# W_in in two parts behind the taps' maximum, block 1's x behind block 0's casts, block 2's first taps on GpSimd

## The chip, the cores and the metric

One core of one Trainium2 chip runs the whole kernel. The metric is the device time in microseconds (us) of one execution.

## The reference, cut to what matters

A causal convolution with seven softmaxed taps per head along the sequence, then a feed-forward layer with exact GELU:

```python
w = softmax(weight)                       # 8 heads x 7 taps
out[b, s, h, :] = sum_k w[h, k] * x_pad[b, s + k, h, :]     # x: 8 x 4096 x 192, 24 columns a head
h = out.reshape(32768, 192) @ w_in        # 192 x 2048
return gelu(h) @ w_out                    # 2048 x 192
```

## The kernel before

Tokens are cut into blocks: six of 256 per half of the sequence, then 512. For each block x is loaded (four DMAs of 96 KB), VectorE transposes it in three parts and applies seven taps (the first a `tensor_scalar`, the other six `scalar_tensor_tensor` with two SBUF inputs), TensorE multiplies by W_in in eight chunks (12 matmuls and one GELU each), ScalarE does the GELU, TensorE multiplies by W_out. Blocks 0 and 1 get their taps on TensorE instead, as matmuls with diagonal matrices that VectorE builds first ("the diagonals"). GpSimd casts, and copies the halo: the few columns that a block needs of the one before. The prologue loads everything through the same 16 DMA engines (from 4 to 5 us of the profile before, W_in's queue took 64.6% of their time and x's 34.3%): block 0's x, W_in (cast to bf16 by GpSimd's DMA queue), block 1's x, W_out, block 2's x.

```python
FP = [0, FQ, 2 * FQ, FH]                  # W_in in three parts: 256, 256, 512 columns of each half
...
# GpSimd
for i in range(3):
    win_in(FP[i], FP[i + 1], S_WIN[i])    # two DMAs each, at once
...
# TensorE, chunk i of block n
if u >= 2: t.wait_ge(S_GELU, u - 1)
...
if n == 0 and i < 3:
    t.wait_ge(S_WIN[i], 32)
...
# the DMA-issuing engine
load(sp, 0, (0, 1))
sp.wait_ge(S_WIN[0], 32)
load(sp, 1)
for i in range(4): ...                    # W_out
load(sp, 2)
load(sp, 3)
```

## Time and profile before

| | value |
|---|---|
| time, median of 3 runs | 683.07 us (682.57 to 683.39) |
| span of the profiled run | 681.6 us |
| TensorE busy | 674.2 us, 99% |
| first matmul of block 2 | 29.91 us |

The lines that bear the argument stand in the prediction. Two more are from the timeline of the kernel before: start, length, engine, line, operation, and in brackets the idle time before it and what ended it.

```profile
9.85 1.27 PE L756 MATMUL hp<-xc,win 64*128 64x256 bf16 x20 [0.17 <-ACT xc L191]
...
21.76 0.88 DVE L548 TENSOR_SCALAR acc<-xT,wcol 128x256 f32<-128x256 f32 x3
22.55 6.02 DVE L555 SCALAR_TENSOR_TENSOR acc<-xT,wcol,acc 128x256 f32<-128x256 f32 x15
```

TensorE runs from its first chunk into its second without waiting for W_in. The fifteen later taps begin at 22.55 us and end at the start of the last three, 28.49, so one comes every 0.396 us, and the third of them starts at 22.55 + 2 x 0.396 = 23.34 us.

### The profile page before, as it was taken

The numbers are of one execution on the slowest core, as the hardware profiler recorded it, in microseconds if no ns is written. First come the engines' busy times: TensorE is split into PE (matmuls) and PEld (weight loads), VectorE is DVE, ScalarE is ACT, GpSimd is POOL, SyncE is SP. The second block draws the span as 40 slices with busy tenths as digits, with TensorE's granted clock in tenths as the row PEclk, the third lists the DMA queues.
The fourth block names the chain that finished last, engine by engine and source line by source line (L and its number), as shares of the span: only waits on it lengthen the run. The fifth ranks groups of instructions, "written<-read, shape, count | busy, mean of one in ns | idle before, by whom it ended". The sixth has DMA issues, their size and how long they took to land.

```text
span 681.6 us, 27311 instructions
## 1 busy us (share of the span) xinstructions
PE 674.2 (99%) x12572; PEld 410.2 (60%) x12572; DVE 560.9 (82%) x908; ACT 536.5 (79%) x548; POOL 38.6 (6%) x57
## 2 busy tenths in 40 slices
PE   7999999999999999999999999999999999999998
PEld 4899755555555555555555555555555555555557
DVE  6899989888889888898888898888898888988611
ACT  6799988877787877777877778777778777778772
POOL 5025100000000000000000000000000000000000
PEclk9999999999999999999999999999999999999999
DMA  9436332234432143432234322334322334221123
GB/s 196 92 101 130 72 71 72 42 78 95 96 93 52 47 95 94 95 73 52 68 94 95 94 64 46 83 94 96 93 48 51 95 94 96 72 46 27 48 50 94
DMA packets 133890, 54.45 MB, mean 80 GB/s; under 512 B 127504, under 2 KB 133776, under 8 KB 133776
## 3 DMA queue, kind: packets, MB, share of 16 engines
q1 hardware_dynamic: 131408, 51.33, 32.0%
q8 instruction: 98, 1.61, 1.0%
q0 software_dynamic: 1248, 0.79, 0.9%
q10 hardware_dynamic: 1120, 0.59, 0.3%
q14 instruction: 16, 0.13, 0.1%
HBM read 28.31 MB, written 25.17 MB: 78 GB/s over the span
## 4 chain that ended last, share of the span: by engine, by line
PE 95%; DMA 2%; DVE 1%; SPq 1%; issue 0%; POOL 0%
PE hp L756 47%; PE ob L818 43%; PE ob L786 5%; DMA xin<-in_x_dram 1%; DVE acc L555 1%; PE hp L786 1%; SPq L330 1%; DMA win<-in_moe_w_in_dram 1%; SPq L882 0%; DVE xT L522 0%; DVE acc L548 0%; DVE xc L555 0%; POOL win L385 0%; POOL idb L393 0%; DVE osb L283 0%
## 5 line engine op out<-in xcount | busy, mean ns | idle before, releaser
L677 ACT ACTIVATE gT<-hp 128x1024 bf16<-128x1024 f32 x512 | 523.1, 1024 | 129.7 <-PE hp L756 126.4
L756 PE MATMUL hp<-xc,win 64*64 64x512 bf16 (+2 forms) x6048 | 419.5, 366 | 2.2 <-DVE xc L555 1.1
L818 PE MATMUL ob<-gT,wout 64*64 64x512 bf16 x5376 | 366.3, 376 | 0.0
L555 DVE SCALAR_TENSOR_TENSOR acc<-xT,wcol,acc 128x512 f32<-128x512 f32 (+1 forms) x495 | 315.3, 708 | 0.0
L756 PEld LDWEIGHTS hp<-xc,win 64*64 64x64 bf16 (+1 forms) x6048 | 189.9, 106 | 135.2 <-ACT gT L677 3.1
L818 PEld LDWEIGHTS ob<-gT,wout 64*64 64x64 bf16 x5376 | 172.0, 118 | 123.0
L314 DVE STREAM_TRANSPOSE osb<-ob 128x512 f32<-128x512 f32 x84 | 74.2, 886 | 100.3 <-PE ob L818 100.3
L522 DVE STREAM_TRANSPOSE xT<-xin 128x512 f32<-128x512 f32 (+1 forms) x105 | 78.4, 807 | 4.5 <-DMA xin<-in_x_dram 4.5
L555 DVE SCALAR_TENSOR_TENSOR xc<-xT,wcol,acc 128x512 bf16<-128x512 f32 (+1 forms) x99 | 65.4, 720 | 0.0
L447 POOL COPY xT<-xT 128x18 f32<-128x18 f32 x30 | 27.9, 930 | 505.0 <-DVE xT L522 482.7
L786 PE MATMUL ob<-wout,gT 64*128 64x192 bf16 x896 | 47.8, 243 | 0.0
L786 PEld LDWEIGHTS ob<-wout,gT 64*128 64x128 bf16 x896 | 40.0, 94 | 3.9 <-issue 0.4
L548 DVE TENSOR_SCALAR acc<-xT,wcol 128x512 f32<-128x512 f32 (+1 forms) x90 | 37.6, 474 | 1.1
L691 PE MATMUL hp<-warm 128*128 128x512 bf16 x12 | 5.1, 616 | 1.3 <-DVE warm L463 1.3
L285 ACT ACTIVATE osb<-ob 128x192 f32<-128x192 f32 x2 | 0.7, 331 | 7.1 <-PE ob L786 7.1
L786 PE MATMUL hp<-wout,gT 64*128 64x192 bf16 x128 | 5.9, 243 | 0.0
L283 DVE COPY osb<-ob 128x192 f32<-128x192 f32 x2 | 0.7, 358 | 6.1 <-PE ob L786 6.1
L786 PEld LDWEIGHTS hp<-wout,gT 64*128 64x128 bf16 x128 | 5.3, 94 | 0.0
L650 ACT ACTIVATE acc<-xT,wcol 128x256 f32<-128x256 f32 (+1 forms) x9 | 5.2, 575 | 0.0
L270 ACT ACTIVATE osb<-ob 128x384 f32<-128x384 f32 x10 | 4.9, 490 | 0.0
L707 PE MATMUL ob<-xTb,dg 64*64 64x256 bf16 (+1 forms) x112 | 3.2, 245 | 1.1 <-ACT xTb L626 1.1
L193 DVE CAST xc<-ob 64x256 bf16<-64x256 f32 (+3 forms) x8 | 2.8, 357 | 1.5 <-PE ob L707 1.4
(36 smaller groups left out, 29.9 us busy)
## 6 DMA issues: line engine op xcount, KB each, us to landing
out_dram<-osb SPq DMA_DIRECT2D x122, 192.0 KB, 3.1
xin<-in_x_dram SPq DMA_DIRECT2D x116, 192.0 KB, 4.1
xin<-in_x_dram SPq DMA_DIRECT2D x22, 96.0 KB, 4.3
woutf<-in_moe_w_out_dram SPq DMA_DIRECT2D x4, 384.0 KB, 6.2
win<-in_moe_w_in_dram POOLq DMA_DIRECT2D x4, 96.0 KB, 3.8
win<-in_moe_w_in_dram POOLq DMA_DIRECT2D x2, 192.0 KB, 5.5
out_dram<-osb SPq DMA_DIRECT2D x8, 48.0 KB, 1.7
out_dram<-osb ACTq DMA_DIRECT2D x4, 96.0 KB, 1.9
```

Source lines behind the costliest of these rows:

```text
L314: v.transpose(ap(osb[m % 2], j, [[8 * C, 128], [C // 2, TB // 32], [NP, 32]]), bank(ring(m, j)),).then_inc(S_EV)
L330: e.dma_start(ap(xin[n % NX], 32 * q * (TB // 32 * DQ), dst), ap(xt, off, src)).then_inc(sm or S_XIN[n % NX], 16)
L447: g.tensor_copy(dst, src).then_inc(S_HALO)
L522: v.transpose(ap(xT[n % 2], p * XW + HX, [[NP * XW, 128], [1, w]]), ap(xin[n % NX], p, [[TB // 32 * DQ, 128], [DQ, w // 32], [NP, 32]],),) ...
L548: ins = v.tensor_scalar(a, src, wk, None, ALU.mult)
L555: ins = v.scalar_tensor_tensor(dst, src, wk, a, op0=ALU.mult, op1=ALU.add)
L650: a.activation(out=acc[n % 2][:, p * TB : p * TB + w], in_=ap(xT[n % 2], p * XW + HX, [[NP * XW, 128], [1, w]]), func=AF.Copy, scale=wcol[ ...
L677: a.activation(out=ap(gT[n % 2], i * c * 2 * w, dst), in_=ap(hp[u % 2], 0, src), func=AF.Gelu,).then_inc(S_GELU)
L691: t.matmul(hp[1][:, 0:512], warm[:, 0:128], warm[:, :])
L756: ins = t.matmul(hp[u % 2][fo : fo + fw, o : o + w], ap(win, f1, [[NP * F, 64], [2, fw]]), xc[n % 2][r, p * TB : p * TB + w], start=(p == ...
L786: ins = t.matmul(bb[sub], gT[m % 2][r, c0 : c0 + 128], wout[r, CH[sub][i] * C : (CH[sub][i] + 1) * C], start=(ph == 0 and i == 0), stop=(p ...
L818: ins = t.matmul(bank(ring(m, j), slice(64 * h, 64 * h + 64), w), ap(wout, 64 * hf * NF * C + CH[h][i] * C + j, [[NF * C, 64], [NP, 64]],) ...
```

## The change

Its intent: let block 0's x have the DMA engines to itself at first (W_in's load waits for `S_PRO`, that is, until VectorE has taken the maximum of the taps, its first step of their softmax), keep block 1's x out of W_in's way, and take three instructions off VectorE, which sets block 2's start.

```diff
-        S_WIN = [sem("S_WIN%d" % i) for i in range(3)]
+        S_WIN = [sem("S_WIN%d" % i) for i in range(2)]
-        FP = [0, FQ, 2 * FQ, FH]
+        FP = [0, FQ, FH]
 # GpSimd
-                    for i in range(3):
+                    g.wait_ge(S_PRO, 1)
+                    for i in range(2):
                         win_in(FP[i], FP[i + 1], S_WIN[i])
...
             for n in range(2, NB):
                 halo(n)
+                if n == KG:               # KG = 2
+                    for p in range(NP):
+                        g.wait_ge(S_TR, NP * n + p + 1)
+                        g.tensor_scalar(acc[...], xT[...], wcol[:, KS - 1 : KS], None, ALU.mult).then_inc(S_KG)
 # VectorE: block KG starts at its second tap
-                if k == h and h:
+                if k == h and n == KG:
+                    v.wait_ge(S_KG, p + 1)
+                elif k == h and h:
 # TensorE
-                if n == 0 and i < 3:
+                if n == 0 and i < 2:
                     t.wait_ge(S_WIN[i], 32)
 # the DMA-issuing engine
-            sp.wait_ge(S_WIN[0], 32)
+            sp.wait_ge(S_CAST[0], NP)
             load(sp, 1)
```

(Cut: the counting of semaphores, GpSimd's wait for the column of taps, and VectorE's wait for the part of W_in that it copies. The call of `tensor_scalar` is shortened.)

More of the change, by code (lines that the diff above doesn't have):

```diff
@@ L36, in bass_lightweight_conv__then__act_gelu_exact_kernel @@
     K0 = {4: 0, 5: 1, 6: 2}
+    KG = 2
     NA = 5
@@ L163, in bass_lightweight_conv__then__act_gelu_exact_kernel @@
         S_K0 = sem("S_K0")
+        S_KG = sem("S_KG")
         block = es.enter_context(nc.Block())
@@ L218, in cvd @@
         def cvd(n):
-            return sum(NCV - NP * (m in K0) for m in range(n + 1) if m not in PC)
+            return sum(NCV - NP * (m in K0 or m == KG) for m in range(n + 1) if m not in PC)
         HC = [0]
@@ L457, in _ @@
                 g.tensor_copy(wout[:, o : o + 4 * C], woutf[:, o : o + 4 * C]).then_inc(S_WOG)
+            g.wait_ge(S_PRO, 9)
             for n in range(2, NB):
                 halo(n)
+                if n == KG:
+                    for p in range(NP):
+                        g.wait_ge(S_TR, NP * n + p + 1)
+                        g.tensor_scalar(
+                            acc[n % 2][:, p * TB : p * TB + WS[n]],
+                            ap(xT[n % 2], p * XW + HX, [[NP * XW, 128], [1, WS[n]]]),
+                            wcol[:, KS - 1 : KS],
+                            None,
+                            ALU.mult,
+                        ).then_inc(S_KG)
         @block.vector
@@ L498, in dup @@
             def dup(s):
-                v.wait_ge(S_WIN[min(s, 2)], 32)
+                v.wait_ge(S_WIN[min(s, 1)], 32)
                 for hf in range(2):
@@ L532, in conv @@
                 w = WS[n]
-                h = int(n in K0)
+                h = int(n in K0 or n == KG)
                 if k == h and p == 0:
@@ L564, in _ @@
                 ops = [] if n in K0 else [("t", n, p) for p in range(NP)]
-                ops += [("c", n, k, p) for k in range(int(n in K0), KS) for p in range(NP)]
+                ops += [("c", n, k, p) for k in range(int(n in K0 or n == KG), KS) for p in range(NP)]
                 if n + 1 in K0:
```

## The prediction

The two terms of its 0.33 us were: about 0.7 us gained if VectorE's later taps run on beside GpSimd's first taps (its "free case", one chance in three), 0.15 if they have to wait for them. Both terms and the chances were estimates, from the times of the taps before (21.76 to 22.55 us) and of GpSimd's taps at 0.45 to 0.5 us each, ending at 22.31 to 22.45. The sum came to 29.91 - 0.33 = 29.58 us for the start of block 2, and so to 682.7 us.

> **What bounds the kernel now.** The page first. It shows an engine that is never free.
>
> ```profile
> PE 674.2 (99%) x12572; PEld 410.2 (60%) x12572; DVE 560.9 (82%) x908; ACT 536.5 (79%) x548; POOL 38.6 (6%) x57
> ...
> PE 95%; DMA 2%; DVE 1%; SPq 1%; issue 0%; POOL 0%
> ```
>
> TensorE is busy for 674.2 of 681.6 us and owns 95% of the chain that ended last. The change touches no matmul, so at most the few us in which TensorE is idle are to be had. Next, who TensorE waited for, over the whole span:
>
> ```profile
> PE hp L691 <- DVE warm L463: 1.3, 1, 1.3
> PE hp L756 <- DVE xc L555: 1.1, 1, 1.1
> PE ob L707 <- ACT xTb L626: 1.1, 1, 1.1
> PE hp L756 <- ACT gT L677: 0.7, 2, 0.5
> PE hp L756 <- ACT xc L191: 0.3, 2, 0.2
> ```
>
> That is the complete list: 4.5 us, all of it in the first 30 us. After 29.91 us TensorE never waits again. So the end moves one for one with the moment at which TensorE starts block 2, and I read only the first 30 us. The chain in order of time, with start, length and what:
>
> ```profile
> 13.02 7.33 DMA xin<-in_x_dram
> 20.37 1.36 DVE xT L522 x3
> ...
> 22.64 4.82 DVE acc L555 x13
> ...
> 29.29 0.49 DVE xc L555
> 29.77 0.14 issue
> 29.91 0.83 PE hp L756 x12
> ```
>
> Block 2's x lands at 20.35 us, VectorE transposes it (1.36 us), does 21 tap instructions, and TensorE starts at 29.91. The timeline of TensorE shows how much this wait is worth:
>
> ```profile
> 28.13 0.66 PE L786 MATMUL ob<-wout,gT 64*128 64x192 bf16 x12
> 29.91 0.29 PE L756 MATMUL hp<-xc,win 64*128 64x256 bf16 x2 [1.12 <-DVE xc L555]
> ```
>
> TensorE is out of work at 28.79 us, 1.12 us earlier. There are thus two paths into 29.91: block 2's (DMA, VectorE), and TensorE's own work on blocks 0 and 1, only 1.12 us shorter. Shortening the first alone gains at most 1.1 us; more needs both shortened.
>
> [...] GpSimd's halo copy of 128x18, 0.31 us when it met first taps or transposes, took 3.56 us at 40.36 us and 11.92 us at 58.14 us, beside runs of later taps. [...] GpSimd's cast takes 0.441 us for 256 columns and 0.826 for 768, a slope of 0.75 ns per column over about 0.25 us. [...] the W_in and x queues share the same engines. The trace agrees: from 4 to 5 us W_in's queue took 64.6% of them and x's 34.3%.
>
> **The change part by part.**
>
> *W_in after the maximum, in two parts.* GpSimd now begins its issues at 2.00 us. The maximum starts at 2.17 and lasts 0.15, so W_in is issued from about 2.35, 0.35 us later. Its packets begin at about 4.0 us now, while block 0's x still has 161 packets to move from 4 to 5 us and 52 from 5 to 6 us. At the 551 packets per us of the slice 3 to 4 us, those 213 take 0.4 us alone. So x of block 0 can land some 0.3 to 0.6 us before its 6.33 us, and no transfer time is lost, as the engines stay full; earlier than 5.25 us helps nothing, as VectorE is busy with the diagonals until then. I take 0.4. Two issues of about 0.65 us go, but the engines, not the issues, are the limit: W_in's 0.79 MB moves at 0.11 to 0.17 MB per us until about 10.5 us either way.
> The price is coarseness. Now piece 1 is there by about 8.4 us (issued from 3.3, 3.7 to 4.3 us to land) and the last piece by 11.2 (5.27 + 5.9). With two parts TensorE's second chunk of block 0 (about 10.2 us now) waits for all of the rest, about 11.0 us. The five gelus from 10.51 us run back to back, each 0.99 us; the second would then start at 11.7 instead of 11.5. Block 0's head start of 0.4 us is spent here, and a further 0.2 may be lost.
>
> *Block 1's x behind the casts.* Its issue waited for W_in's first part (6.64 us); it will wait for ScalarE's third cast, which ends at 8.14 now and at 7.75 if x lands 0.4 earlier: 1.1 us later. But its packets didn't flow from 6.66 on: x's queue moved one packet from 6 to 9 us, W_in all the rest. They moved from 9 to 12 us. Issued 1.1 us later they find W_in nearly done. I expect block 1's x at 13.1 us instead of 12.74. GpSimd's casts of it end 1.5 us after landing for the second third, and TensorE's taps (14.30 us) waited 0.21 us for just that cast, so they follow: TensorE's own path ends at 28.79 + 0.4 = 29.2 us.
> W_out and block 2's x are issued behind it, about 1.1 us later too. Block 2's x was issued 7.3 us before it landed; it stood in a queue that was over 90% full from 3 to 20 us. The same bytes through the same full engines: I leave 20.35 us, plus or minus 0.5.
>
> *First taps on GpSimd.* Three VectorE instructions go. They stood from 21.76 to 22.55 us, so up to 0.79 us, if the later taps may start at once. GpSimd, as with block 1's casts (0.59 us after the first transpose begins, then 0.45 each), would run them at 20.96, 21.41 and 21.86 and end at 22.31; with fp32 output and a scalar per partition perhaps 0.5 each, ending at 22.45. VectorE's first later tap is ready at 21.76, in the middle. [...] I give the free case one chance in three: 0.33 x 0.7 + 0.67 x 0.15 = 0.33 us.
> The later taps cost the same: 18 at 0.40 us.
>
> *Sum.* Block 2's path: 29.91 - 0.33 = 29.58. TensorE's path: 29.2. The later one counts: 29.58, a gain of 0.33 us, so 683.07 - 0.33 = 682.7 us. Block 3 follows on VectorE without a break (its last tap ends at 40.30, TensorE wants it at 40.44), so the same gain is passed on, no more.
>
> **The rivals.** *1: all as intended.* The casts and taps on GpSimd overlap cleanly, block 2's x lands 0.3 us earlier. For it: engines full, bytes the same. Against it: the 11.92 us halo copy. Then 29.91 - 0.79 - 0.3 = 28.82 and TensorE's path at 29.2 becomes the bound: 682.4; with that path also shorter by its 0.4 us head start, 681.9. *2: block 1's x is the new wait.* It lands 1.1 us later, as it is issued; TensorE's path then ends at 29.9, and the time stays at 683.1 whatever GpSimd does. For it: TensorE waited for exactly this cast. Against it: the queue's idle time from 6 to 9 us. *3: GpSimd's taps are slow*, 0.7 us each and shut out by VectorE: the third ends at about 23.8, the third later tap starts 0.4 us later than now: 683.5. *4: W_out slips.* Its last part landed at 18.8 us, and TensorE wants it, cast (0.83 us), at about 20.5: 1 us of slip makes TensorE wait and delays GpSimd's first taps, 683.6.
>
> **Range and chances.** The middle is 682.7. Rival 1 at 681.9 and rivals 3 and 4 at 683.6 bound it, and the runs before spread over 0.8 us by themselves: 681.8 to 683.7 should hold it 8 times in 10. A change of 2% is 13.7 us. All idle time of TensorE together is 4.5 us, so faster by 2% isn't possible, and a loss of that size would need a stall in the steady part, which the change doesn't touch: 0.01 for each.
>
> **What would show it.** In the changed profile: transposes of block 0 start at about 5.95 us rather than 6.35; block 0's second gelu starts near 11.7; block 1's transposes start near 13.1, block 2's near 20.4; the three GpSimd taps take about 0.5 us each, with a wait of VectorE's first or third later tap for them; TensorE's wait before block 2 shrinks from 1.12 us to about 0.4; no new wait of TensorE after 31 us. I am wrong if block 2's x lands over 0.6 us away from 20.35, if the GpSimd taps take over 0.7 us, or if TensorE's wait moves to block 1's taps or to W_out.

## The result, and the profile after

The changed kernel took 684.06 us in the median of 6 runs (682.97 to 685.06), the kernel before 683.34 in 6 runs beside it. The ratio is 1.0012, 95% interval 0.9999 to 1.0025: 2% is far off either way, but 684.06 lies outside the predicted 681.8 to 683.7, and the small change points the other way than predicted. That it is a loss at all is nearly, not quite, clear of noise: the interval just includes no change, and so does that of the same kernel in e9, 1.0007 (0.9994 to 1.0019). (A ratio is the mean time of one kernel's fast runs over that of the other's of the same rounds, so not quite the ratio of the medians quoted.)

The profiled run took 683.77 us, with a span of 682.0. First again who TensorE waited for, in the changed kernel; columns as in the prediction: total, times, longest.

```profile
PE hp L774 <- DMA win<-in_moe_w_in_dram: 1.5, 1, 1.5
PE hp L709 <- DVE warm L479: 1.3, 1, 1.3
PE hp L774 <- DVE xc L573: 0.9, 1, 0.9
PE hp L774 <- ACT xc L194: 0.5, 2, 0.3
PE hp L774 <- ACT gT L695: 0.5, 1, 0.5
```

The wait for ScalarE's cast of block 0 (1.1 us before) is gone, as intended. A wait of 1.5 us for W_in has taken its place, and the wait before block 2 is still 0.9. The chain in order of time shows why that one remains:

```profile
20.32 0.54 DVE xT L538
...
20.95 0.77 POOL acc L469
...
21.87 1.82 POOL acc L469 x2
...
23.72 4.12 DVE acc L573 x11
...
30.29 0.83 PE hp L774 x12
```

Block 2's x is there at 20.30 us, as before, and as predicted. But VectorE now waits for GpSimd: the three taps end at 23.69, and VectorE's third later tap starts at 23.72 instead of 23.34. TensorE starts block 2 at 30.29 instead of 29.91, 0.38 us later. The end follows: span less start of block 2 is 682.0 - 30.29 = 651.71, before 681.6 - 29.91 = 651.69. In this profile the GpSimd taps account for the whole 0.4 us by which its span is longer. The timeline shows the GpSimd taps, and VectorE beside them:

```profile
20.95 2.73 POOL L469 TENSOR_SCALAR acc<-xT,wcol 128x256 f32<-128x256 f32 x3 [1.22 <-DVE xT L538]
...
22.02 0.59 DVE L573 SCALAR_TENSOR_TENSOR acc<-xT,wcol,acc 128x256 f32<-128x256 f32 x1 [0.35 <-POOL acc L469]
...
22.82 0.69 DVE L573 SCALAR_TENSOR_TENSOR acc<-xT,wcol,acc 128x256 f32<-128x256 f32 x1 [0.20 <-POOL acc L469]
```

A tap takes 0.91 us on GpSimd (three in 2.73), where 0.5 was predicted.

It looked settled. One thing did not fit: this profiled run had a mean TensorE clock of 1.000, while the five others of the same kernel had 0.997 to 0.998, and four of these five were slower than it. A part of the loss in the medians was in runs of which there was no trace yet.

### The profile page after: what moved, and what is told of

Read it like the earlier page. It is cut to its first block, busy times and chain, and to the rows that moved or that the text cites. A ratio compares the mean times of both kernels' runs of the same rounds, so it can differ in the third digit from the quotient of the medians.

```text
span 682.0 us, 27309 instructions
## 1 busy us (share of the span) xinstructions
PE 674.3 (99%) x12572; PEld 417.2 (61%) x12572; DVE 561.1 (82%) x905; ACT 535.9 (79%) x548; POOL 40.0 (6%) x58
## 4 chain that ended last, share of the span: by engine, by line
PE 95%; DVE 1%; DMA 1%; SPq 1%; POOL 0%; issue 0%; ACT 0%; ACTq 0%
PE hp L774 47%; PE ob L836 43%; PE ob L804 5%; DMA xin<-in_x_dram 1%; PE hp L804 1%; DVE acc L573 1%; SPq L333 0%; POOL acc L469 0%; SPq L901 0%; DMA wsb<-in_weight_dram 0%; ACT xTb L644 0%; DVE xT L538 0%; DVE xc L573 0%; DVE wcol L501 0%; DVE dg L507 0%
## 5 line engine op out<-in xcount | busy, mean ns | idle before, releaser
L774 PEld LDWEIGHTS hp<-xc,win 64*64 64x64 bf16 (+1 forms) x6048 | 193.3, 106 | 133.1 <-ACT gT L695 2.7
L836 PEld LDWEIGHTS ob<-gT,wout 64*64 64x64 bf16 x5376 | 175.6, 118 | 119.5
L518 DVE COPY win<-win 64x768 bf16<-64x768 bf16 x8 | 3.4, 420 | 2.1 <-DMA win<-in_moe_w_in_dram 1.8
```

What stands on the lines that cost most here:

```text
L774: ins = t.matmul(hp[u % 2][fo : fo + fw, o : o + w], ap(win, f1, [[NP * F, 64], [2, fw]]), xc[n % 2][r, p * TB : p * TB + w], start=(p == ...
L836: ins = t.matmul(bank(ring(m, j), slice(64 * h, 64 * h + 64), w), ap(wout, 64 * hf * NF * C + CH[h][i] * C + j, [[NF * C, 64], [NP, 64]],) ...
```

## The experiments

Twelve runs, each beside the kernel before on the same chip. The label's first part (e1, e2, ...) is its name in the text.

### e1 to e4: one part undone, or one part alone

e1: the changed kernel with `KG = -1`, so that block 2's first taps are VectorE's again.

```diff
-    KG = 2
+    KG = -1
```

> The changed kernel with only block 2's first taps put back on VectorE. Theory T (the loss is made by the GpSimd taps, 0.91 us each instead of the 0.5 that was predicted): block 2's last tap ends where it did before, near 29.8 us, TensorE's own path stays at 29.4, and the time falls to that of the kernel before within 0.2 us (ratio 1.000). Rival L (the loads make the loss, by landing block 2's x or W_out later in most runs): the time stays 0.4 to 0.8 us over the kernel before (ratio about 1.001).

Measured: 684.27 us, ratio 1.0014 (1.0001 to 1.0027). **Theory T fell.** The taps were gone and the loss stayed. Mean clock 1.000 in its profile, 0.995 to 0.997 in its four other runs. Its profile shows block 2's x late, at 21.32 us, which alone sets that run's end, so the rival L was alive as well.

e2: the kernel before with only the GpSimd taps (the lines of the diff with `KG`, nothing of the loads).

> The kernel before with only block 2's first taps on GpSimd, W_in in three parts at once and block 1's x behind W_in's first part as before. Theory T: three taps of 0.91 us in a row, the third later tap near 23.7 us, TensorE's wait before block 2 grows from 1.1 to 1.5 us, time 0.4 us over before (ratio 1.0006). Rival L: ratio 1.000 or below.

Measured: 684.16 us, ratio 1.0011 (0.9999 to 1.0023); clock 1.000 in all five. From e2's timeline:

```profile
20.93 1.35 DVE L537 STREAM_TRANSPOSE xT<-xin 128x256 f32<-128x256 f32 x3 [2.14 <-DMA xin<-in_x_dram]
21.57 2.73 POOL L468 TENSOR_SCALAR acc<-xT,wcol 128x256 f32<-128x256 f32 x3 [1.12 <-DVE xT L537]
...
24.33 5.24 DVE L572 SCALAR_TENSOR_TENSOR acc<-xT,wcol,acc 128x256 f32<-128x256 f32 x13 [0.20 <-POOL acc L468]
```

From the first transpose to VectorE's third later tap it is 24.33 - 20.93 = 3.40 us; in the changed kernel 23.72 - 20.32 = 3.40; in the kernel before 23.34 - 20.37 = 2.97. So the taps cost block 2's path 0.43 us. The measured 0.8 us is more, but its interval holds 0.4, and none. In e2's profile block 2's x was also 0.56 us later than in the profile before (20.93 against 20.37), and TensorE waited 1.7 us for W_in's third part. Theory T's account of the taps stands in the traces, as one cause.

e3: the kernel before with only W_in in two parts behind the maximum.

```diff
 # from the changed kernel
-    KG = 2
+    KG = -1
-            sp.wait_ge(S_CAST[0], NP)
+            sp.wait_ge(S_WIN[0], 32)
```

> The kernel before with only W_in changed: two parts, issued after the maximum; block 1's x still waits for W_in's first part. Block 0's transposes start near 5.35 us (1.0 us earlier), but its second gelu waits for the rest of W_in until 12 us. Theory T: block 2's path does not change, ratio 1.000. Rival L: some tenths of a us slower.

Measured: 684.01 us, ratio 1.0011 (0.9997 to 1.0026); clock 0.995 to 0.997 in four of six runs. Its profile is one with the low clock (0.997), and TensorE never waited for block 2's taps in it: they end at 28.59 + 1.27 = 29.86 us, but TensorE gets to block 2 only at 31.10. This is where the next theory came from. The stretches of that profile; the columns are from and to, length, busy time of TensorE, its weight loads, VectorE, ScalarE and GpSimd with their instructions, then TensorE's granted clock, DMA share and GB/s:

```profile
10.00:12.00 2.00, 0.00 (x0) 0.00 (x0) 0.00 (x0) 0.63 (x1) 0.00 (x0) 1.00 1.13 242
...
13.00:14.00 1.00, 0.65 (x12) 0.29 (x6) 0.94 (x3) 1.00 (x2) 0.00 (x0) 0.72 1.06 354
14.00:15.00 1.00, 0.93 (x10) 0.69 (x12) 1.00 (x3) 0.93 (x2) 0.50 (x2) 0.50 1.07 376
...
16.00:17.00 1.00, 1.00 (x16) 0.53 (x16) 0.15 (x1) 0.74 (x2) 1.00 (x2) 0.58 1.18 229
```

TensorE does nothing from 10 to 12 us (no W_in). After it resumes, its clock goes to 0.50 for some three us.

e4: the kernel before with only the other gate for block 1's x.

```diff
-            sp.wait_ge(S_WIN[0], 32)
+            sp.wait_ge(S_CAST[0], NP)
```

> The kernel before with only block 1's x issued behind block 0's casts (near 8.2 us instead of 6.7). Block 1's x lands 0.5 to 1.2 us later, TensorE's own path ends by that much later, at 29.3 to 30.0 us. Theory T: block 2's x still lands near 20.3, ratio 1.000 to 1.0003. Rival L: block 2's x and W_out land up to 1 us later, ratio 1.001 or more.

Measured: 683.92 us, ratio 1.0007 (0.9995 to 1.002), clock 1.000 in all. In its profile block 1's transposes start at 13.39 us (12.76 before), the last matmuls ahead of block 2 at 28.68 (28.13 before), block 2's x is there at 20.37. So TensorE's own path grows by 0.55 us and stays hidden in that run. Whether this part costs anything by itself is not resolved.

### e5 to e8: the clock, the tap, and block 2's x

e5: e1 with matmuls on zeros in TensorE's wait.

```diff
+                if n == 0 and i == 1:
+                    for _ in range(8):
+                        t.matmul(hp[1][:, 0:512], warm[:, 0:128], warm[:, :])
                 if n == 0 and i < 2:
                     t.wait_ge(S_WIN[i], 32)
```

> As e1_taps_back (both load changes, first taps on VectorE; 684.3 us, clock 0.995 to 0.997 in four of five runs), plus eight idle matmuls on TensorE between block 0's first and second chunk, where it waits for the rest of W_in. Theory C (the wait of 1.5 to 2.6 us lets TensorE's clock fall to half for about 3 us, which lengthens TensorE's own path until that path sets the end): clock 1.000 in all runs, time 683.3 to 683.7, so 0.6 to 1.0 us below e1. Rival X (in those runs block 2's x lands late, as in e1's own profile, at 21.3 us; the clock is beside the point): clock 1.000, time still about 684.3.

Measured: 683.25 us, ratio 0.9995 (0.9983 to 1.0008), clock 1.000 in all five runs. Against e1's 1.0014 the loss is gone, though on another chip. Its profiled run is its slowest, 684.57 us, and there block 2's x landed at 21.6 us with a full clock: rival X also exists, as scatter. The filler is not free either: in that profile VectorE used W_in's last part from 11.32 us, TensorE, still busy with the zeros, from 11.64.

e6: three kinds of tap one after another. Its output is wrong, which doesn't matter for the time.

```diff
+                        if p == 0:   gi = g.tensor_scalar(ga, gx, wcol[:, KS - 1 : KS], None, ALU.mult)
+                        elif p == 1: gi = g.tensor_scalar(ga, gx, 1.0, None, ALU.mult)
+                        else:        gi = g.tensor_copy(ga, gx)
-                    v.wait_ge(S_KG, p + 1)
+                    v.wait_ge(S_KG, NP)
```

> The changed kernel with three different instructions in place of the three equal GpSimd taps (wrong result on purpose): the scalar from a column, the scalar as a constant, and a plain copy; VectorE's later taps wait for all three, so that no later tap runs beside them. Theory T (a tap costs 0.91 us by itself, for its multiply with a scalar): first 0.91, copy about 0.45. Rival P [...]: all three near 0.45 to 0.5, for now only transposes run beside them.

Measured, one look, 685.27 us. From its timeline:

```profile
22.20 0.93 POOL L472 TENSOR_SCALAR acc<-xT,wcol 128x256 f32<-128x256 f32 x1 [0.93 <-DVE xT L540]
23.11 0.84 POOL L474 TENSOR_SCALAR acc<-xT 128x256 f32<-128x256 f32 x1
23.91 0.39 POOL L476 COPY acc<-xT 128x256 f32<-128x256 f32 x1
```

With no later tap of VectorE beside them, the multiply still takes 0.93 us and the copy of the same size 0.39. VectorE's transposes ran beside the first until 22.92 us, but beside the second (0.84) and the third VectorE did nothing. So VectorE's work beside it, the suspicion of rival P, is not what makes a tap slow; the multiply is. Taking the scalar from the column is the least of it: 0.09 us, by one instruction each.

e7: the kernel before with block 2's x ahead of the second half of W_out.

```diff
                 ).then_inc(S_WOUT[i], 16)
+                if i == 1:
+                    load(sp, 2)
-            load(sp, 2)
             load(sp, 3)
-            share = {1: [4, 12, 9, 9, 10, 5, 5, 6]}
+            share = {1: [4, 0, 12, 12, 12, 8, 6, 6]}
```

> The kernel before with block 2's x issued ahead of W_out's third and fourth part, and the W_out matmuls that need those parts moved one chunk later. If block 2's x sets the end (theory X2), it lands near 18.5 us and TensorE's wait before block 2 goes; the end is then TensorE's own path with a new wait for W_out of up to 0.7 us: time 0.3 to 1.0 us below before, and its runs scatter less. Rival: W_out slips by the 1.9 us that block 2's x takes and TensorE waits for it over 1 us: time as before or above.

Measured: 684.76 us, ratio 1.0012 (0.9999 to 1.0024): the rival. Who TensorE and VectorE waited for, from e7's timeline:

```profile
18.91 1.35 DVE L522 STREAM_TRANSPOSE xT<-xin 128x256 f32<-128x256 f32 x3 [1.01 <-DMA xin<-in_x_dram]
...
23.38 1.16 PE L786 MATMUL ob<-wout,gT 64*128 64x192 bf16 x24 [1.48 <-POOL wout L457]
23.50 6.03 DVE L555 SCALAR_TENSOR_TENSOR acc<-xT,wcol,acc 128x256 f32<-128x256 f32 x15 [1.77 <-POOL xT L447]
```

Block 2's x is 1.5 us earlier. But TensorE now waits 1.48 us for GpSimd's cast of W_out, and VectorE 1.77 us for a halo copy which stands behind that cast in GpSimd's order.

e8: the kernel before with block 3's x held back.

```diff
             load(sp, 2)
+            sp.wait_ge(S_XIN[2], 64)
             load(sp, 3)
```

> The kernel before with block 3's x issued only when block 2's has landed. If the traffic behind block 2's x delays it (its packets had moved by 18 us, its last part landed at 20.35), it lands 0.5 to 1.5 us earlier and the time falls by up to 1.1 us. If the engines serve it in order and what follows does not matter, it lands at 20.3 and the time stays within 0.3 us of before.

Measured: 682.63 us, ratio 0.9986 (0.9972 to 0.9999). It is faster than the kernel before, by most of what was hoped, though of thirteen versions compared one interval that just misses 1 can be chance. Its profile doesn't show how: that run is the second slowest of five (683.45), and block 2's x landed in it at 20.4 us.

### e9 to e12: the two causes on one chip

e9 is the changed kernel again, unaltered.

> The changed kernel once more, unaltered, as the yardstick for the three beside it: about 684 us, ratio about 1.001; mean clock 0.995 to 0.998 in most runs, where TensorE waited for the rest of W_in. Its trace is wanted in a run with the low clock: there TensorE should run at half rate for about 3 us between 13 and 17 us, and start block 2 without waiting for VectorE.

Measured: 684.14 us, ratio 1.0007 (0.9994 to 1.0019); clock 0.997 or 0.998 in all five. Its trace is the one that was wanted. First its stretches (columns as for e3), then its chain in order of time:

```profile
10.00:12.00 2.00, 0.63 (x10) 0.54 (x12) 0.63 (x2) 0.35 (x1) 0.00 (x0) 0.93 1.17 279
12.00:13.00 1.00, 1.00 (x14) 0.71 (x12) 0.94 (x3) 0.42 (x1) 0.00 (x0) 0.50 1.10 272
13.00:14.00 1.00, 1.00 (x12) 0.56 (x10) 0.60 (x3) 0.74 (x2) 0.00 (x0) 0.50 0.95 335
14.00:15.00 1.00, 1.00 (x14) 0.52 (x10) 0.97 (x4) 0.88 (x1) 0.87 (x3) 0.50 1.05 383
15.00:16.00 1.00, 1.00 (x22) 0.69 (x24) 0.74 (x2) 0.84 (x1) 1.00 (x2) 0.94 1.09 374
```

```profile
4.70 6.62 DMA win<-in_moe_w_in_dram
...
11.37 4.47 PE hp L774 x48
15.84 0.89 PE ob L725 x28
...
29.76 0.49 PE ob L804 x12
30.26 0.66 PE hp L774 x12
```

The chain no longer runs through block 2's x, VectorE or GpSimd at all. It runs from W_in's landing, over 48 matmuls that take 4.47 us, into TensorE's own work. In the first profile of the same kernel, at full clock, the first 24 of these took 1.49 us and the next 24, with a wait for the GELU of 0.47 us before them, 1.74. By the timeline e9 starts block 2 at 30.09 us, although its taps were done at 28.46 + 1.27 = 29.73.

e10: the changed kernel, GpSimd taps and all, plus e5's eight matmuls.

> The changed kernel with the eight idle matmuls in TensorE's wait for W_in; the taps stay on GpSimd. Theory C plus T (two causes, on two paths that meet before block 2): clock 1.000 in all runs; what is left is the taps' 0.43 us, so ratio 1.0003 to 1.0008, between the changed kernel and e11. If only the clock mattered: as e11. If only the taps did: as the changed kernel.

Measured: 683.41 us, ratio 0.9997 (0.9984 to 1.0009), clock 0.999 or 1.000 in all. The same part of its timeline:

```profile
9.29 1.90 PE L760 MATMUL hp<-warm 128*128 128x512 bf16 x8
11.93 1.49 PE L777 MATMUL hp<-xc,win 64*128 64x256 bf16 x24 [0.74 <-DMA win<-in_moe_w_in_dram]
13.88 1.75 PE L777 MATMUL hp<-xc,win 64*128 64x256 bf16 x24 [0.47 <-ACT gT L695]
```

W_in came even later than in e9 (11.93 against 11.37 us), and still the 48 matmuls were over sooner, at 15.63 against 15.84. The means of e9 and e10 are 684.13 and 683.44 us, a difference of 0.7 with two standard errors of 0.5. The kernels differ by the filler alone: this is the clock's share, less what the filler itself costs.

e11: e5's kernel again.

> The same kernel as e5_keep_warm, on one chip with the others: both load changes, no GpSimd taps, idle matmuls. Both causes are gone: clock 1.000, ratio 0.999 to 1.0002.

Measured: 683.39 us, ratio 0.9997 (0.9984 to 1.0009), clock 0.999 or 1.000. The times of e10 and e11 do not tell the taps apart; the theory of two causes expected 0.4 us between them, and that failed. The traces, of one run each, offer a reason: in e10 the taps end at 28.63 + 1.27 = 29.90 us, and TensorE's own path has grown to 30.04 in its chain, so that both meet. Removing the taps leaves TensorE's path, which sets the start in e11's profile too. That the taps cost 0.43 us of the time, and not only of block 2's path, is thus argued from the traces of the changed kernel and e2; no pair of times shows it.

e12: e11 with e8's hold.

> e11 with block 3's x issued only when block 2's has landed, which alone gave ratio 0.9986 (e8). The candidate for a version that beats both kernels: if the two add up, ratio about 0.998 to 0.9985; if block 2's x is not sped up by the hold but merely less scattered, about 0.999.

Measured: 683.14 us, ratio 0.9992 (0.9979 to 1.0006). Block 2's x was there at 19.00 us in its profile, block 2 started at 28.99, and its span of 680.7 us is the shortest of all profiles. In the median it is no better than e8, and not clear of the noise. Of the versions tried only e8, the kernel before with one wait more, has an interval below 1, and only just.

All profiles but those of e6 and e7, in us: block 2's first transpose, end of its last tap, start of block 2 on TensorE, and which of the two paths sets it.

| kernel | x transposed from | taps end | block 2 starts | set by | clock |
|---|---|---|---|---|---|
| before | 20.37 | 29.76 | 29.91 | taps | 1.000 |
| changed | 20.32 | 30.15 | 30.29 | taps | 1.000 |
| e1 | 21.34 | 30.74 | 30.88 | taps (late x) | 1.000 |
| e2 | 20.93 | 30.75 | 30.90 | taps | 1.000 |
| e4 | 20.37 | 29.76 | 29.90 | taps | 1.000 |
| e5 | 21.62 | 31.01 | 31.15 | taps (late x) | 1.000 |
| e8 | 20.45 | 29.84 | 29.98 | taps | 1.000 |
| e9 (changed) | 19.91 | 29.73 | 30.09 | TensorE | 0.997 |
| e3 | 20.48 | 29.86 | 31.10 | TensorE | 0.997 |
| e10 | 20.08 | 29.90 | 30.05 | both | 1.000 |
| e11 | 19.87 | 29.25 | 29.43 | TensorE | 1.000 |
| e12 | 19.00 | 28.38 | 28.99 | TensorE | 1.000 |

In each row the span is 651.7 us more than the start of block 2, to within 0.05 (e9: 681.8 - 30.09 = 651.71; e12: 680.7 - 28.99 = 651.71). What precedes it decides everything.

## Why the prediction was wrong

It named the right place (the join of two paths before block 2, with 1.12 us between them) and the right rule (the end moves one for one with it). Both terms of its sum came out higher than predicted. (Two readings beside it were loose and changed nothing: TensorE's idle time is 681.6 - 674.2 = 7.4 us, the 4.5 us of the list and a tail of 2.9 behind the last matmul; and rival 1's last time is 682.0 by its own sum, not 681.9.)

**The step "perhaps 0.5 each" for the GpSimd taps failed.** It was an estimate that put the multiply a little above the cast's 0.441 us; GpSimd runs no multiply of that kind in the kernel before that could have shown it. The multiply takes 0.91 to 0.93 us, over twice the copy's 0.39 (e6). So the term "0.33 us gained" is 0.43 us lost (e2), and block 2's path lets TensorE start at 30.29 in the profile, not 29.58. Rival 3 had slow taps, 0.7 us each and shut out by VectorE (a supposition, from the halo copy of 11.92 us), with the third ending at about 23.8. It ended at 23.69, but by luck: each took 0.91 us, and they ran back to back (20.95 + 2.73), shut out by nothing. Nor did VectorE have to wait until a GpSimd instruction was over, as the prediction feared: its two taps of 22.02 to 22.61 and 22.82 to 23.51 us ran wholly inside GpSimd's second and third, at 0.59 and 0.69 us instead of about 0.49, and then waited for the next GpSimd tap anyway.

**The step "Block 0's head start of 0.4 us is spent here, and a further 0.2 may be lost" failed,** not in naming the wait for W_in but in what it does. It was treated as a delay that ends when W_in lands. In the trace TensorE's clock was halved after it (0.50 from 12 to 15 us in e9). In e9 TensorE resumes at 11.37 us, after a wait of 2.1. Two short stretches of that profile hold the fall and the return:

```profile
11.60:11.80 0.20, 0.20 (x8) 0.19 (x4) 0.17 (x2) 0.00 (x0) 0.00 (x0) 0.77 0.96 198
...
15.10:15.20 0.10, 0.10 (x6) 0.07 (x2) 0.10 (x1) 0.04 (x1) 0.10 (x1) 0.89 0.96 353
```

The slice before them has a clock of 1.00, those between 0.50, the one behind 1.00. If the clock stepped once in each of the two, 0.77 in the first means half rate in 0.46 of its 0.2 us, so from 11.71 us on, and 0.89 in the second half rate in 0.22 of its 0.1, so until 15.12. By this estimate it was half rate for 3.41 us; in e3, in the same way (0.59 from 13.4 to 13.6 us, 0.88 from 16.8 to 17.0), from 13.44 to 16.85, 3.41 us again. Why it lasts so long, and why one run loses its clock and the next does not, no trace here shows: the profiled runs of e1 and e6 waited 1.8 and 2.3 us for W_in and kept a clock of 1.000, those of e9 and e3 waited 2.1 and 2.6 us and lost it. Half rate for 3.41 us of 681.8 also gives the mean clock of the run, 1 - 0.5 x 3.41 / 681.8 = 0.9975; by the same sum a mean of 0.995 would be two such stretches. Of the 22 runs of kernels with W_in in two parts and no filler (changed, e1, e3, e9), 18 had a mean clock of 0.998 or below; of the 20 with filler, none. The times follow the clock: over all of these runs, whatever their chip, the 4 runs at 1.000 average 683.76 us, the 16 at 0.997 or 0.998 684.08, and the 2 at 0.995 took 685.37 and 685.70 (a later W_in, with its longer wait, may do part of that itself; e10 against e9 is the test). The three-part kernels e2, e4, e7 and e8 kept 1.000 in 20 runs, and the kernel before fell to 0.998 in one of the 29 runs with a clock on record, though the profiles of e2, e4, e7 and e8 show waits of 0.8 to 1.7 us for W_in: there TensorE has a second chunk to work on before it waits. That this is what keeps the clock is argued, not tested.

What it costs can be estimated. In the changed kernel's first profile TensorE took up W_in's rest at 11.30 us and began its last matmuls before block 2 at 28.76; e10, at full clock, took it up 0.63 later and began them 0.62 later, at 29.38. By this e9 (taken up at 11.37) would have begun them at 28.83, but it did at 29.60: the halved clock adds some 0.77 us to TensorE's path, which is also what its 48 matmuls took longer (4.47 us against 3.70 from 11.30 to 15.00). Of that the whole kernel pays only what sticks out behind the taps, in e9 about 0.2 us (30.09 against 29.73 and the 0.14 that TensorE took to start behind the taps in the first profile). In e3 wait and clock together stick out by 1.1 (31.10 against 29.86 and 0.14).

The diff's coarser W_in was the hint: of the new wait on TensorE it should have been asked what it does to the clock.

Point by point, against what the prediction said would show it:

- Block 0's transposes from 5.95 us: they start at 5.35, a head start of 1.0 us, larger than thought. Part of it is scatter: the profiles of e2, e4, e7 and e8, whose W_in is that of the kernel before, start at 5.73 to 6.19, not 6.35.
- Its second GELU near 11.7 us: 12.18. The rest of W_in landed at 11.3, not 11.0, and TensorE waited 1.5 us for it; its issues began at 2.81 us, not 2.35. The head start bought nothing.
- Block 1's x at 13.1 us: 13.29. Near, but partly by luck: by the chain it was issued at 7.16 us, 0.5 later than before and not 1.1, and landed 0.5 later, so that the full queue hid none of the delay there. In e4 it was issued 1.05 later and landed 0.63 later. TensorE's path, measured at its last matmuls before block 2, is 28.76 - 28.13 = 0.63 us longer; 0.4 was predicted. These are single profiles: in e2 and e8, with W_in and block 1's x as in the kernel before, the same matmuls start at 29.41 and 28.98.
- Block 2's x at 20.35 us, plus or minus 0.5: 20.30. Right for the profiled runs, but over the profiles the transposes begin anywhere from 19.9 to 21.6 us (without e7, e8 and e12, which touched that load or the one behind it), and this scatter blurs every time here.
- The GpSimd taps about 0.5 us each, and VectorE's first or third later tap waiting for them: 0.91, and all of the first three waited (0.35, 0.20 and 0.20 us). The prediction's own sign of being wrong, taps over 0.7 us, came true; a wait for W_in was not among its signs.
- TensorE's wait before block 2 about 0.4 us: 0.87, as 1.12 - 0.63 + 0.38, the shifts of the two paths.
- No new wait after 31 us: right.

Why undoing one part never restored the time: the end is the later of two paths. The GpSimd taps lengthen one (0.43 us), the wait for W_in with its half clock the other (e9: start of block 2 at 30.09 with the taps done at 29.73). e1 removes the first and keeps the second; e2 keeps the first without the second; by their medians each loses most of the whole, though e1's profile lost its time to a late x. What stays open: whether block 1's later x costs anything alone (e4), how much of the wait for W_in the coarser split makes and how much its scatter (its last part was used first at 10.7 to 12.1 us in the nine profiles of kernels with two parts), and through what e8 gains.

## What to carry to other kernels

A new wait on TensorE can cost more than its length (here an estimated 3.41 us at half clock behind waits of 2.1 and 2.6 us, in the profiles of e9 and e3): look at the granted clock run by run, not only in the profiled run, before explaining a small loss. Where two paths meet, undoing one cause of two leaves the time as it was, so test them with the other one removed. Before moving an instruction to an idle engine, get that engine's time for that very operation: on GpSimd the copy took 0.39 us and the multiply of the same size 0.84 to 0.93 (on VectorE 0.35, on average for the six of that size in the kernel before).
